# Both halves of an inverse transform copied out of PSUM in one step, with a new order of all operations

## The chip, the cores and the metric

The kernel runs on one core of a Trainium2 chip. The metric is the device time in microseconds (us) of one execution. The engines are TensorE (PE in the profile, its weight loads PEld), VectorE (DVE), ScalarE (ACT), GpSimd (POOL) and SyncE (SP). PE writes its results to PSUM, which has eight banks; every result has to be copied out by ACT or DVE before its bank can be used again.

## The reference

Sparse attention (8 global keys and a local window of 96) is followed by a gated long convolution that is computed with a Fourier transform along the sequence. Shapes: q, k, v are 4 x 8 x 768 x 64, the output is 4 x 768 x 512.

```python
scores = scale * q @ k^T - slope[h] * distance      # only kept keys: pos < 8, or 0 <= rel < 96
a = softmax(scores); x = (a @ v) as [B, S, 512]
x1, x2, x3 = split(x @ w_proj)                      # 512 columns each
conv = irfft(rfft(x2, axis=seq) * rfft(filter, axis=seq))
out = (x1 * conv * x3) @ w_out
```

## The kernel before

The work goes batch by batch, four of them; while one batch is in its convolution, the next is in its attention. Per batch the stages are:

- load q and k (DMAs that GpSimd issues, L347), turn them with TensorE (L704, L707; operations "q" and "k") and copy the result to QT and KT (L322);
- scores of two heads (a head pair) against a group of two or three key tiles (L756, operation "scores"). The contraction is over 64 rows, so two matmuls, one on each half of the array, go side by side. A group is evacuated by one ACT exponential (L771) from two banks and, except in batch 0, multiplied by a mask on DVE (L788). In batch 0 each group also has a bias matmul over 128 rows ahead of it (L750, operation "near");
- values (L806, L811), division by the row sum (L830 on DVE or L834 on ACT, into xn), transposition (L852) and a copy to xT (L322);
- gates: x1 and x3, from xT and w (L932; copies L326 or L942, product L946);
- projection of the folded sequence (L997; copies to ab, L322), forward transform (L1163; copies to X), products with the filter's transform (L1181 to L1201);
- inverse transform, `conv`, L1028 and L1035: for each of four column tiles a matrix for the even part and one for the odd part, four matmuls of 128 columns each (operation "inv"). Each goes to a bank of its own, 384 columns wide, and is copied to the tile `eo` (L322);
- recombination on DVE (L1120 to L1126, `mixed`), then the gate (L1140 to L1145, `gated`), the output projection (L1090, operation "out"), its copy to `ot` (L326 or L328) and the store.

`Plan` records some 980 operations with what they read, write and hold. Nothing is scheduled at run time: the string `ORDER` (L41) lists all operations as number, engine letter (P, A, V, G, S) and, for those that take PSUM banks, the banks' numbers. `i2` with a bank is a filler of two matmuls without use (L318). `Plan.schedule` follows the list, so each engine's queue is what the list says, and an engine that waits for its next operation does nothing else. With each operation the list also chooses between ACT and DVE where both can do it.

What the program joins in one step is told by tuples of batch numbers: with `PAIR_X` two banks of the forward transform are copied by one instruction of 1024 columns, and with `PAIR_EO` the even and the odd half of an inverse would be copied by one instruction of 768 columns. `PAIR_EO` is empty, so there are 32 copies of 384 columns. The lines that take the one way or the other (in `conv`):

```python
both = [g.bank(), g.bank()] if b in self.PAIR_EO else None
...
g.op("P", ..., turn, acq=[bk] if not both else () if par else both, use=[bk] if both and par else (), ...)
if both and par == 0:
    continue
if both:
    g.op("AV", self.evac(2 * h), lambda e, ...: self.copy(e, eo[:, jj], both[0].two()[:, :, 0:h]), use=both, ...)
    continue
g.op("AV", self.evac(h), lambda e, ...: self.copy(e, eo[:, jj, par], bk.f32()[:, 0:h]), use=[bk], ...)
```

Of the kernel before, what the change touches and what calls it, by code (L numbers as in the profile page):

```python
# [42 lines left out]
50G 82P0 19V 12A 23V 58S 34G 57V 49A 47V 51G 24V 80P6 52G 35V 25A 86P2 13V 71G 20A 14V 81A 83V 60G 198P7 15A 36A 62G
41A 92P0 203V 200V 37V 59G 87V 94P1 79A 64G 202V 43A 206V 84P6 93A 63G 199V 96P45 95V 76A 61G 88P0 201A 97A 205V
146P23 85V 65G 74A 90P1 204V 40A 42V 39A 102P45 91V 89A 152P67 147A 38V 28V 115P01 103A 26V 207V 98P23 153A 27V 208V
236G 100P45 99A 209V 148P67 233G 116A 119P23 210V 149A 231G 211V 120A 104P01 235G 117P67 212V 101A 230G 105V 113P23
106V 118A 232G 150P45 213V 114A 107P67 234G 124P01 151A 108V 109V 154P23 229G 72A 214V 110P5 66G 111P 125V 73A 155V
121P67 126V 221P4 242G 30A 156V 159P01 222A 67G 122V 77A 157P2 112V 335P3 238G 158A 160V 217P4 123V 215P5 336A 240G
161V 127P2 333P6 218A 128P 237G 334V 329P3 216A 219P0 129V 241G 75A 331P6 330V 369P45 220A 162P1 332V 244G 134P7
370A 163V 239G 366P23 189V 345P01 136A 130P4 346A 190V 243G 223P67 191V 367A 68G 192V 226P01 193V 135P5 227A 451G  # L50
347V 228A 348P23 194V 165P0 132V 245G 349A 137V 131P1 78A 69G 195V 337P2 350V 225A 403P45 70G 181V 164P3 224A 338V
456G 404A 341P7 180V 168P2 248G 342A 182V 169P6 133V 170A 183V 249G 406P45 166A 371V 343P1 407A 339P7 184V 251G
142P2 171V 344A 340V 138P3 250G 246S 167V 144A 409P67 247S 412P45 252G 185V 410A 351P01 186V 139P2 187V 450G 352A
140V 143P6 196V 413A 172P7 141V 353V 375P01 174A 372P23 414V 354P45 373A 253G 255P7 188V 368V 376A 267P2 462G 197V
256A 411V 457G 259P1 355A 377V 374V 463G 257P7 268A 356V 260A 405V 279P45 452G 258A 280P 357P23 145V 281A 378P01
408V 455G 269P7 358V 379V 359A 380V 453G 381P45 282V 261P01 458G 262P 382V 271P6 383V 263A 454G 283V 360P23 272A
176P4 471G 264V 270A 555P5 361V 265V 178A 470G 415P01 556A 362V 273P67 461G 274P 416V 173P4 417V 275A 464G 551P5
549P2 175V 552A 363P3 465G 550V 364P 420P01 276V 365A 460G 586P45 277V 565P67 587A 459G 384P2 421V 385P 266V 177P3
566A 254G 422V 561P4 553P5 386A 693G 418P6 278V 623P01 419A 423P7 562V 674G 395P2 424A 179V 298P6 685G 554V 624A
563P4 391P7 442V 397A 683G 396P3 299A 441V 564A 557P5 466G 294P0 398V 387P1 558A 443V 682G 286P2 559P3 393A 444V  # L60
568P45 287A 681G 560V 399P6 295A 569A 288P0 445V 592P23 290P7 588V 389A 392P4 671G 593A 570V 400P1 446V 677G 291A
394V 296P5 401A 429P2 447V 297A 472G 289A 589P67 402V 284P3 431A 686S 473G 292P5 449V 590A 388P4 448V 469G 574P01
285A 632P67 567V 293A 468S 489P2 633A 689G 625V 467S 390V 425P3 575A 680G 591V 626P45 427A 571P67 301V 433P0 474G
627A 672S 300V 437P1 687S 572A 634V 684G 426P3 673S 302V 490A 675G 595P45 576V 439A 629P67 596A 475P2 303V 676G 573V
435A 491P1 304V 678G 630A 594V 580P45 476A 305V 670G 438P0 492A 581V 487P2 631V 582A 688G 440V 577P67 428V 691G
493P01 494P 597V 479P3 488A 306V 679G 495A 499P45 578V 628V 500P 477P2 501A 307V 598P01 478A 579V 601P45 690G 480A
599V 583P7 502V 600A 584P 430P6 602V 692G 771S 603V 434P2 503V 773S 481P45 585A 482P 432V 604P3 605P 308V 635P01
483A 769S 640P67 496V 606A 636V 314P4 497V 768S 637A 641V 485V 311P5 642V 770S 619P3 498V 607P6 315A 777S 436V 638P7
312A 514P0 484V 615P1 621A 309V 639A 643P2 317P3 775S 617A 486V 515A 518P7 644A 506P1 310V 516P0 510P4 609A 774S
504P2 519A 508P5 662V 620P6 505A 318A 616P7 661V 772S 507A 781P23 509A 618V 608P1 511A 663V 779S 782A 512P7 320P5  # L70
622V 513A 610V 517A 780S 784P23 664V 790P67 321A 657P0 521V 785A 611P1 778S 665V 659A 808P45 520V 791A 323P3 776S
666V 809A 522V 787P67 645P0 324A 792V 313S 788A 706P5 523V 667V 613A 805P23 783V 802P67 707A 612P1 668V 803A 326P4
789V 647A 614V 806A 849P67 524V 846P01 694P5 850A 669V 807V 847A 852P23 710P6 525V 695A 804V 327A 708P7 526V 711A
328S 810V 811P01 853A 325S 843P45 851V 696P6 319S 709A 529V 316S 844A 796P23 322S 698P7 797V 812A 854V 798V 712P45
713P 699A 718P01 786V 719P 697A 653P2 530V 720A 700P67 701P 646P3 813V 714A 848V 649P1 648V 655A 860P45 702A 527V
793P23 651A 654P0 861V 721V 862A 658P1 794V 656V 817P67 795V 543P0 660V 818V 845V 546P1 819A 722V 814P23 528V 855P45
547A 815V 703V 537P6 816A 856V 704V 799P7 800P 857V 650P1 801A 863P2 715V 820P3 858P4 864A 821P 705V 531P5 859A 716V
822A 735P2 652V 723P4 534P7 717V 724A 544A 727P1 886V 725P4 736A 737P3 545S 733P0 532A 834P2 885V 548S 726A 839P5
728A 887V 738A 729P4 734A 731P1 888V 838P3 730A 732A 889V 823P0 840A 739V 890A 828P4 740V 906P1 836A 891V 825A 894P2
538A 741V 892V 540P0 742A 893V 866P3 830A 743V 907A 896P6 541A 744V 898P4 895A 542S 745V 897A 539S 918P01 535A 748V  # L80
919P 533S 908P2 899A 536S 746V 920A 900P67 901P 829P4 749V 902A 910P0 921V 909A 871P1 911A 903V 912P67 841A 904V
913P 833P0 914A 922V 824P2 905V 831A 865P5 835A 916V 826A 923P4 942P7 915V 938P0 943A 927P2 762P6 917V 924A 928A
842V 925P4 939A 747V 929P2 926A 870P7 930A 837V 944P4 940P0 932V 945A 750P2 931V 941A 933V 763A 756P4 946V 751A 947V
832V 934A 765P0 948V 827V 949A 935V 753P2 757A 936V 950V 867A 880P6 758S 951V 873A 937V 754A 876P4 952V 766A 953V
759P5 755S 882A 752S 955V 868A 875P0 767S 954V 760A 764S 956V 881P6 877A 761S 968V 878A 957P1 872A 966V 883A 879V
963P0 958A 874V 869V 884V 960P5 959S 964A 967V 969V 965S 974P4 961A 975P 962S 970P1 976A 971P 977S 978P0 972A 979P
# [1258 lines left out]
```

## Time and profile before

| | |
|---|---|
| time, median of 3 runs | 164.04 us (164.03 to 164.37) |
| the profiled execution's own time | 163.79 us |
| its span, first to last instruction | 162.0 us |
| PE busy | 153.5 us, 1587 matmuls |
| DVE busy | 151.2 us, 358 instructions |
| ACT busy | 153.6 us, 318 instructions |
| POOL busy | 77.1 us, 101 instructions |
| mean granted TensorE clock | 0.997 |

A busy time counts an instruction from its start to its end, and neighbours on one engine overlap: what an instruction costs its engine is the distance from its start to the start of the next. In the timeline a row merges neighbours of one form: the first column is the start of the first, the second the time until the end of the last, xN their number. The distance between two rows' first columns, divided by N, is then the cost of one. In the list of waits the columns are the total, the number and the longest wait in us; a wait of PEld for "issue" is one that no semaphore explains.

### The profile page before, as it was taken

What the parts mean: (1) busy time and instruction counts of PE and PEld (TensorE: products, weight loads), DVE (VectorE), ACT (ScalarE), POOL (GpSimd) and SP (SyncE); (2) the same over time, 40 slices, a digit from 0 to 9 for tenths busy, and PEclk for the clock granted to TensorE, in tenths of its full rate; (3) what the DMA queues carried; (4) which work ended last, traced back from release to release, by engine and by line L of the source; (5) the groups of instructions that cost most, each with busy time, mean ns of one, the idle gap of its engine ahead of it and who ended that gap; (6) DMA issues with size and microseconds to landing.
All of it is one profiled execution on the core that took longest, in us unless ns stands there. A gap on an engine that the chain in (4) does not pass through costs nothing.

```text
span 162.0 us, 4215 instructions
## 1 busy us (share of the span) xinstructions
PE 153.5 (95%) x1587; PEld 92.7 (57%) x1587; DVE 151.2 (93%) x358; ACT 153.6 (95%) x318; POOL 77.1 (48%) x101
## 2 busy tenths in 40 slices
PE   4879899999999999999999999999999999999990
PEld 1564238756656687764568565445666754574550
DVE  6799898999999999999999999999999999999941
ACT  7999899999999999999999999999999999999970
POOL 7999199989978999999971000000000000000000
PEclk9999999999999999999999999999999999999998
DMA  4999999999999999999999984707000303300775
GB/s 169 213 154 148 168 150 152 153 158 165 178 165 150 136 137 138 154 153 163 163 94 152 103 160 99 121 13 296 27 4 6 129 0 126 135 4 0 302 282 195
DMA packets 84956, 21.95 MB, mean 135 GB/s; under 512 B 75584, under 2 KB 81992, under 8 KB 84936
## 3 DMA queue, kind: packets, MB, share of 16 engines
q0 software_dynamic: 73040, 12.11, 104.5%
q1 hardware_dynamic: 11896, 9.57, 22.4%
q8 instruction: 12, 0.20, 0.5%
q14 instruction: 8, 0.07, 0.1%
HBM read 25.40 MB, written 6.29 MB: 196 GB/s over the span
## 4 chain that ended last, share of the span: by engine, by line
PE 86%; ACT 4%; POOL 3%; issue 2%; DVE 1%; POOLq 0%
PE bank L932 26%; PE bank L997 13%; PE bank L1090 12%; PE bank L756 7%; PE bank L806 4%; PE bank L852 4%; PE bank L811 4%; PE bank L1028 3%; PE bank L704 3%; PE bank L1163 3%; PE bank L750 3%; ACT mask L624 1%; PE bank L1035 1%; POOL qn L347 1%; PE bank L687 1%
## 5 line engine op out<-in xcount | busy, mean ns | idle before, releaser
L932 PE MATMUL bank<-xT,w 128*128 128x384 f16 x256 | 48.6, 326 | 0.0
L771 ACT ACTIVATE E<-bank 128x864 f16<-128x864 f32 x48 | 42.0, 930 | 0.9 <-PE bank L756 0.8
L932 PEld LDWEIGHTS <-w 128*128 128x128 f16 x256 | 23.3, 98 | 15.7 <-issue 1.6
L347 POOL DMA_DIRECT2D vn<-in_v_dram x28 | 25.7, 937 | 2.0 <-DMA w<-in_moe_w_proj_dram 0.9
L347 POOL DMA_DIRECT2D kn<-in_k_dram x25 | 21.7, 886 | 4.6 <-DMA vn<-in_v_dram 3.6
L1090 PE MATMUL bank<-wo,y 128*128 128x512 f16 (+1 forms) x100 | 23.0, 370 | 0.0
L347 POOL DMA_DIRECT2D qn<-in_q_dram x25 | 22.1, 891 | 1.0 <-PE bank L673 0.5
L788 DVE TENSOR_TENSOR E<-E,mask 128x864 f16<-128x864 f16 x36 | 20.7, 596 | 0.0
L326 ACT ACTIVATE x<-bank 128x384 f16<-128x384 f32 x30 | 16.5, 552 | 0.1
L997 PE MATMUL bank<-w,xs 128*128 128x512 f16 x64 | 16.0, 379 | 0.0
L322 ACT CAST eo<-bank 128x384 f16<-128x384 f32 x32 | 15.3, 594 | 0.5 <-ACT g L942 0.3
L326 ACT ACTIVATE ot<-bank 128x512 f32<-128x512 f32 x23 | 14.7, 665 | 1.0 <-PE bank L1090 1.0
L756 PE MATMUL bank<-QT,KT 64*128 64x216 f16 (+2 forms) x224 | 15.2, 245 | 0.0
L806 PEld LDWEIGHTS <-E 128*128 128x128 f16 x224 | 13.9, 97 | 2.0 <-issue 0.2
L806 PE MATMUL bank<-vn,E 128*128 128x65 f16 x224 | 14.9, 193 | 0.0
L811 PE MATMUL bank<-vn,E 128*128 128x65 f16 x192 | 14.7, 193 | 0.0
L834 ACT ACTIVATE xn<-bank,rc 128x64 f16<-128x64 f32 x64 | 14.1, 407 | 0.2 <-DVE rc L835 0.2
L1090 PEld LDWEIGHTS <-y 128*128 128x128 f16 x100 | 9.2, 98 | 8.7 <-issue 0.2
L322 ACT CAST ab<-bank 128x512 f16<-128x512 f32 x24 | 14.0, 628 | 0.0
L756 PEld LDWEIGHTS <-KT 64*128 64x128 f16 x224 | 7.6, 94 | 11.2 <-issue 10.0
L811 PEld LDWEIGHTS <-E 128*128 128x128 f16 x192 | 13.1, 97 | 0.6
L830 DVE TENSOR_TENSOR xn<-bank,rc 128x512 f16<-128x512 f32 (+1 forms) x17 | 13.0, 776 | 0.2
(158 smaller groups left out, 329.9 us busy)
## 6 DMA issues: line engine op xcount, KB each, us to landing
out_dram<-ot SPq DMA_DIRECT2D x23, 256.0 KB
vn<-in_v_dram POOLq DMA_DIRECT2D x28, 120.0 KB, 7.7
kn<-in_k_dram POOLq DMA_DIRECT2D x16, 96.0 KB, 5.1
qn<-in_q_dram POOLq DMA_DIRECT2D x16, 96.0 KB, 5.1
w<-in_moe_w_proj_dram POOLq DMA_DIRECT2D x4, 256.0 KB, 5.8
kn<-in_k_dram POOLq DMA_DIRECT2D x7, 120.0 KB, 6.8
g<-in_moe_filter_fft_dram POOLq DMA_DIRECT2D x1, 768.0 KB, 9.9
qn<-in_q_dram POOLq DMA_DIRECT2D x6, 128.0 KB, 7.9
```

The lines of the kernel that those rows point to most:

```text
L322: {"A": nc.scalar.copy, "V": nc.vector.tensor_copy, "G": nc.gpsimd.tensor_copy}[e](out, in_)
L326: self.nc.scalar.mul(out, in_, c)
L347: return self.g.op(eng, 0.57 + 0.00035 * nbytes[0] if eng == "G" else 0.5, lambda _: e.dma_start(dst, src), w=w, r=r, nbytes=nbytes, name= ...
L756: nc.tensor.matmul(bs[hh].f32()[:, off:off + w], self.KT[hs, hp, P * m:P * m + P], self.QT[hs, hp, KL * m:KL * m + w], start=(off == 0 and ...
L771: g.op("A", act(864), lambda _: nc.scalar.activation(eo, bs[0].two()[:, :, 0:432].rearrange("p h (m w) -> p h m w", m=2), Act.Exp, scale=s ...
L788: g.op("V", dve(864, 2), lambda _: nc.vector.tensor_mul(eo, eo, mk), r=[("mask", 2 * hp), ("mask", 2 * hp + 1)], w=[("E", hp, gi)], name=" ...
L806: nc.tensor.matmul(o[:, n, hh], ef[:, at:at + P], vt[:, t, 2 * hp + hh, 0:D + 1], start=first, stop=(t == 0), skip_group_check=True)
L811: nc.tensor.matmul(o[:, n, hh], ef[:, at:at + P], vt[:, t - 1, 2 * hp + hh, 0:D + 1], start=False, stop=True, skip_group_check=True)
L834: nc.scalar.mul(to[:, i, n], o[:, i, n, 0:D], rc[:, i, n])
L932: nc.tensor.matmul(bk.f32()[:, 0:h], self.w[:, c, o + P * j:o + P * j + P], self.xT[:, c, h * s:h * s + h], start=(c == 0), stop=(c == 3))
L997: nc.tensor.matmul(bk.f32(), src[:, c], w[:, c, DM:2 * DM], start=(c == 0), stop=(c == 3))
L1090: nc.tensor.matmul(bk.f32()[:, 0:n], y[:, c, P * t:P * t + P], self.wo[:, c, cs], start=(c == 0), stop=(c == 3))
```

## The change

`PAIR_EO` holds all four batches now: the first inverse matrix of a pair takes both banks, the second writes to the other one, and one instruction of 768 columns copies both. So 32 copies of 384 columns become 16 of 768, and sixteen operations fall away. `ORDER` was made anew for that; the planner that made it (it isn't part of the kernel) now counts DVE's waits behind GpSimd's DMA issues. The list is one line shorter, so a line of the kernel after has a number lower by one.

```diff
 ORDER = """
-44S 3G 1V 4V 46S 31G 5V 0V 55S 2A 8A i2b0 9V 48S 7V 10A 16P6 54G 32V 21P1 45A 53G 17A 11P7 6G 18V 22A 33V 56A 29V
...
+44S 3G 1V 4V 46S 31G 5V 0V 21P5 55S 2A 29A 8V 48S 16P4 7V 22A 30V 11P2 54G 17A 23V 45A i2b1 53G 24V 12A 33V 6G 18V
...
     PAIR_X = (0,1,2,3)
-    PAIR_EO = ()
+    PAIR_EO = (0,1,2,3)
     PAIR_OT = ()
```

PE keeps its 1587 matmuls and GpSimd and SyncE keep the order of all their instructions. What moves is the order on PE, ACT and DVE, the banks, and the choice between ACT and DVE: ACT has 19 instructions fewer, DVE 4 fewer. Among them ACT takes four QT copies and two KT copies more, and three copies to xT, two fillings of E with constants and one scaling xn (eight instructions, L834) fewer; DVE has the other side of each.

The first place is PE in the attention of batch 3. In the rows, L756 (L755 after) is a matmul of scores with its weight load, L932 (L931 after) one of a gate; `bank_105` to `bank_108` are the four pairs of banks. Before:

```order
L932 LDWEIGHTS w
L932 MATMUL bank_108<-xT,w 128x384
L756 LDWEIGHTS KT
L756 MATMUL bank_106<-QT,KT 128x216
L756 LDWEIGHTS KT
L756 MATMUL bank_106<-QT,KT 128x216
L756 LDWEIGHTS KT
L756 MATMUL bank_106<-QT,KT 128x216
L756 LDWEIGHTS KT
L756 MATMUL bank_106<-QT,KT 128x216
L932 LDWEIGHTS w
L932 MATMUL bank_105<-xT,w 128x384
```

One group of scores stands alone between gates. After, at the end of the first run of scores in that attention:

```order
L755 LDWEIGHTS KT
L755 MATMUL bank_106<-QT,KT 128x216
L755 LDWEIGHTS KT
L755 MATMUL bank_106<-QT,KT 128x216
L755 LDWEIGHTS KT
L755 MATMUL bank_108<-QT,KT 128x216
L755 LDWEIGHTS KT
L755 MATMUL bank_108<-QT,KT 128x216
L755 LDWEIGHTS KT
L755 MATMUL bank_108<-QT,KT 128x216
L755 LDWEIGHTS KT
L755 MATMUL bank_108<-QT,KT 128x216
```

Here the group in `bank_106` is followed by the one in `bank_108` with nothing between. Over the whole of PE's order, the 36 groups of scores of batches 1 to 3 stand in 23 runs before and in 17 after: 7, 8 and 8 in the three batches before, 7, 5 and 5 after.

The second place is ACT at the inverse transform of the last batch. `eo<-bank` is the copy of an inverse, `ot<-bank` one of an output, `uw<-uw` a step of the recombination. Before:

```order
L942 CAST g_88<-bank_106 128x384
L322 CAST eo<-bank_108 128x384
L322 CAST eo<-bank_107 128x384
L322 CAST eo<-bank_106 128x384
L322 CAST eo<-bank_105 128x384
L322 CAST eo<-bank_107 128x384
L322 CAST eo<-bank_106 128x384
L322 CAST eo<-bank_107 128x384
L322 CAST eo<-bank_105 128x384
L326 ACTIVATE ot<-bank_108 128x512
L326 ACTIVATE ot<-bank_106 128x512
```

After:

```order
L941 CAST g_88<-bank_107 128x384
L325 ACTIVATE x_94<-bank_107 128x384
L941 CAST g_88<-bank_105 128x384
L321 CAST eo<-bank_106 128x768
L321 CAST eo<-bank_107 128x768
L321 CAST eo<-bank_108 128x768
L321 CAST eo<-bank_105 128x768
L325 ACTIVATE uw<-uw 128x4x128
L325 ACTIVATE ot<-bank_107 128x512
```

Eight copies have become four, each from another pair of banks, and the recombination's step now comes right behind them.

The third place is the head of ACT's queue. `E<-uw` fills a part of E with constants, `vn<-uw` a part of vn with ones; `y<-bank` is the first step of the sine tables, `kn<-h`, `qn<-h` and `kn<-pp` are casts of the first loads. Before:

```order
L444 ACTIVATE warm<-warm 1x2
L337 ACTIVATE E<-uw 128x2x6x32
L337 ACTIVATE E<-uw 128x2x80
L337 ACTIVATE E<-uw 128x2x6x32
L337 ACTIVATE E<-uw 128x2x80
L322 CAST kn<-h_85 128x768
L491 ACTIVATE y<-bank_108 128x256
L491 ACTIVATE y<-bank_105 128x512
L322 CAST vn_63<-X 8x8x64
L491 ACTIVATE y<-bank_108 128x512
L322 CAST kn<-pp 128x768
L501 ACTIVATE fold<-y 128x512
```

After:

```order
L443 ACTIVATE warm<-warm 1x2
L336 ACTIVATE vn_63<-uw 128x8x32
L336 ACTIVATE vn_63<-uw 128x48x2
L490 ACTIVATE y<-bank_107 128x512
L490 ACTIVATE y<-bank_107 128x256
L321 CAST kn<-h_85 128x768
L490 ACTIVATE y<-bank_106 128x512
L500 ACTIVATE fold<-y 128x512
L321 CAST qn<-h_86 128x768
L500 ACTIVATE fwd<-y 128x256
L325 ACTIVATE eo<-ident 128x128 x2
L321 COPY p_84<-fwd 128x512
```

The tables' steps now come ahead of most casts and of all fillings of E, which went to DVE.

More of the change, by code (lines that the diff above doesn't have):

```diff
@@ L41 @@
 ORDER = """
-44S 3G 1V 4V 46S 31G 5V 0V 55S 2A 8A i2b0 9V 48S 7V 10A 16P6 54G 32V 21P1 45A 53G 17A 11P7 6G 18V 22A 33V 56A 29V
[L43 to L86, printed above, removed]
@@ L87 @@
-982P7 980V 983P 973S 984V 981S 985S
+44S 3G 1V 4V 46S 31G 5V 0V 21P5 55S 2A 29A 8V 48S 16P4 7V 22A 30V 11P2 54G 17A 23V 45A i2b1 53G 24V 12A 33V 6G 18V
+25A 19V 50G 82P1 47A 13V 32V 34G 20A 80P0 38A 51G 41A 26A 198P4 14V 52G 83A 36V 92P5 56V 71G 15A 204V 58S 200V 49V
+81A 60G 35V 86P7 37A 10V 62G 39V 96P01 203V 27V 59G 206V 73A 84P6 64G 201V 72A 202V 57V 9V 93A 113P23 63G 199V 205V
+42V 97A 90P4 87V 61G 94P5 114A 88P0 65G 85V 91A 89V 98P23 76A 115P67 95V 43A 99A 148P01 116A 40V 152P45 28V 207V
@@ new lines @@
+149A 208V 236G 100P23 77A 102P01 209V 233G 153A 150P67 210V 103A 119P45 231G 211V 151A 104P01 235G 212V 120A 146P67
+105V 230G 106V 101A 117P45 213V 232G 147A 107P01 234G 121P23 118A 108V 214V 154P67 229G 74A 122V 109V 219P4 66G 78A
+110P5 123V 111P 223P01 220A 242G 155V 112V 159P23 224A 156V 67G 225A 124P45 75A 215P0 238G 125V 160V 331P1 126V 216A
+226P67 240G 161V 332A 329P4 127P5 128P 237G 330V 157P0 227A 325P1 158V 228A 162P2 241G 129V 327P4 326A 217P0 180V
+244G 134P5 163A 328V 218A 221P1 239G 190V 136A 399P67 362P23 181V 222A 243G 130P0 189V 400A 182V 68G 341P45 131P1
@@ new lines @@
+132A 191V 447G 363A 183V 164P0 192V 342A 245G 344P67 193V 135P2 133V 345A 69G 364V 402P45 337P1 194V 403A 70G 333P7
+195V 168P6 137V 166A 452G 169P3 338A 184V 248G 185V 170A 365P45 196V 339P2 334A 171V 335P6 249G 165P0 197V 366A 336V
+142P3 251G 340A 167V 138P5 246S 250G 346V 144A 371P67 247S 186V 140A 350P23 252G 401V 368P01 372A 139P4 187V 351A
+446G 367V 143P5 141V 369A 172P6 145V 347P23 404V 174A 408P45 405P01 188V 79A 253G 267P6 370V 348A 343V 458G 255P7
+406A 373V 453G 349V 257P3 256A 407V 409A 459G 353P01 352V 259P2 268A 354V 410V 258A 448G 279P45 355V 280P 356P67
@@ new lines @@
+281A 451G 269P3 357V 358V 260A 449G 377P01 282V 270A 261P45 262P 454G 378V 283V 374P67 263A 541P2 379V 450G 271P3
+542A 375V 264V 467G 547P0 376V 272A 173P1 548A 466G 265V 273P45 274P 175V 411P67 275A 457G 266V 359P2 543P1 460G
+412V 276V 360P 544A 416P45 413V 461G 176P3 361A 456G 417V 277V 557P01 578P67 178A 418V 380P2 455G 579A 381P 177P3
+278V 254G 558A 615P45 414P7 179V 685G 419P6 616A 415V 287P01 288P 382V 545P3 420A 284P45 617V 666G 285P 289A 395P2
+437V 286A 293P67 677G 294P 438V 555P0 397A 290P45 546A 675G 291P 383P1 559V 295A 440V 553P2 462G 551P3 385A 439V
@@ new lines @@
+387P6 554A 674G 552V 391P1 292A 441V 673G 392P2 393A 296V 384P4 389A 663G 394V 556A 549P5 386V 560P67 669G 618P23
+442V 550A 624P01 297V 421P4 561A 468G 443V 483P5 423A 678S 298V 469G 619A 396P6 445V 465G 625A 471P4 398V 464S 580V
+484A 681G 563P67 463S 621P01 444V 472A 566P23 388P5 672G 564A 299V 626V 487P4 567A 470G 565V 429P6 664S 390V 622A
+676G 300V 679S 422P7 488A 623V 665S 667G 581P01 431A 584P23 301V 587P45 582A 485P6 668G 562V 588A 424V 475P0 670G
+583V 486A 302V 433P1 585A 662G 568V 569P45 476A 489P67 589V 680G 490P 435A 572P23 570V 586V 491A 473P0 683G 573V
@@ new lines @@
+571V 574A 430P1 492V 425P6 620V 671G 590P45 303V 427A 495P23 474A 496P 593P67 591V 432V 497A 426P0 594V 592V 682G
+434P1 595A 428V 477P23 304V 478P 684G 759S 632P45 436V 479A 575P0 761S 576P 633V 498V 596P1 597P 577A 627P67 493V
+757S 499V 598A 307P3 628V 634V 629A 313P0 756S 481V 310P2 480V 758S 599P1 305V 635P4 314A 630P5 482V 601A 603P6 765S
+636A 494V 611P7 631A 306V 607P0 308A 763S 311A 608P1 654V 613A 509P45 609A 510P 653V 506P23 605A 762S 507P 612P0
+511A 610V 500P67 508A 655V 501P 760S 503P45 504P 656V 502A 316P1 614V 505A 767S 772P23 657V 778P67 317A 600P0 513V
@@ new lines @@
+779A 768S 322P5 512V 773A 602V 645P4 658V 766S 323A 796P01 780V 775P23 647A 769P67 659V 797A 637P5 764S 514V 604P4
+776A 798V 638P0 770A 515V 309S 606V 793P23 324S 639A 516V 790P67 794A 698P4 640V 791A 517V 649P5 777V 699A 840P01
+831P23 660V 651A 799P67 686P4 841A 518V 661V 832A 319P5 792V 800A 688P0 842V 320A 521V 834P23 689A 837P67 321S 702P1
+771V 687A 315S 835A 801V 312S 710P45 711P 522V 318S 690P0 703A 838A 833V 784P23 700P1 836V 691A 839V 712A 692P67
+785V 693P 795V 538P0 701A 786V 694A 704P45 774V 705P 848P23 519V 539A 781P67 706A 843P01 849V 782V 520V 850A 646P4
@@ new lines @@
+783V 535P5 648V 696V 805P67 650P4 844V 806V 536A 695V 802P23 807A 537S 845V 529P5 540S 803V 652V 846P0 641P1 804A
+708V 642P4 713V 707V 851P7 787P6 643A 788P 714V 808P2 852A 809P 526P1 847V 810A 697V 523P0 789A 709V 724P23 644V
+527A 725P 718P67 874V 719P 726A 854P1 720A 873V 721P23 722P 827P4 856A 875V 723A 715P67 716P 876V 811P1 717A 877V
+822P2 829A 727V 878A 882P6 728V 894P3 530A 879V 883A 729V 859P4 895A 880V 906P67 730A 907P 532P3 881V 908A 731V
+886P5 732V 813A 884P6 887A 733V 824A 898P1 885A 736V 861A 888P67 533A 889P 909V 896P2 890A 534S 737V 869P4 531S 897A
@@ new lines @@
+891V 826P3 899A 892V 900P67 828A 901P 816P1 910V 902A 893V 750P5 524A 903V 812P6 871A 525S 904V 818A 821P4 528S 751A
+905V 817P0 814A 823A 734V 914P23 819A 915P 911P45 912P 825V 916A 927P01 815V 924P67 820V 925P 735V 928P 913A 863P2
+926A 917V 753P3 830V 929A 918V 738P4 919V 930V 920A 858P5 931V 739A 932V 744P6 921V 933A 922V 754A 741P0 934V 860A
+923V 935V 745A 853P4 937V 742A 746S 747P1 936V 855A 743S 939V 864P0 740S 748A 938V 755S 868P4 940V 752S 950V 941P1
+749S 870A 862V 866A 857V 947P6 872V 865A 952V 942A 944P5 867V 948A 951V 943S 953V 949S 958P7 945A 959P 946S 954P4
@@ L88 @@
+960V 955P 962P7 961S 956A 963P 966P3 964V 967P 957S 968A 965S 969S
 """
```

## The prediction

> **What bounds the kernel now.** I read the page first, then the list of waits by stage, then PE's timeline. The page's first part and its chain:
>
> ```profile
> span 162.0 us, 4215 instructions
> PE 153.5 (95%) x1587; PEld 92.7 (57%) x1587; DVE 151.2 (93%) x358; ACT 153.6 (95%) x318; POOL 77.1 (48%) x101
> ...
> PE 86%; ACT 4%; POOL 3%; issue 2%; DVE 1%; POOLq 0%
> ```
>
> Three engines look equally full, so the shares decide nothing; the chain gives 86% of the span to PE. To test that, I asked for PE's own waits between 20 and 158 us. The answer has its heading and not one row. What is left stands with its weight loads, whose first row in the same stretch is by far the largest:
>
> ```profile
> PEld L756 <- issue: 7.5, 21, 0.4
> ```
>
> So from 20 us on PE waits for nobody. Its only gaps lie around the scores (L756), and no semaphore explains them. ACT in turn waits for PE there, which is how an engine looks that has room:
>
> ```profile
> ACT E L771 <- PE bank L756: 0.8, 2, 0.6
> ```
>
> The end is therefore: the time at which PE has become dense, plus PE's work from there, plus a tail. The tail:
>
> ```profile
> 155.69 2.55 PE L1090 MATMUL bank<-wo,y 128*128 128x512 f16 x15
> 157.89 0.80 DVE L328 TENSOR_SCALAR ot<-bank 128x256 f32<-128x256 f32 x2 [2.23 <-ACT ot L326]
> ```
>
> PE ends at 155.69 + 2.55 = 158.24, the span at 162.0: 3.8 us for the last copies and stores, whose pieces the new list keeps. What saves time must shorten PE's work or make PE dense sooner. 1 us is then 1 us.
>
> **Part 1: fewer runs of scores.** PE's timeline gives the price of a run:
>
> ```profile
> 36.36 1.47 PE L932 MATMUL bank<-xT,w 128*128 128x384 f16 x8
> 37.67 0.50 PE L704 MATMUL bank<-ident,qn 128*128 128x128 f16 x6
> ...
> 97.17 0.36 PE L756 MATMUL bank<-QT,KT 64*128 64x216 f16 x4
> 97.46 0.82 PE L932 MATMUL bank<-xT,w 128*128 128x384 f16 x4
> ...
> 99.30 0.54 PE L756 MATMUL bank<-QT,KT 64*128 64x216 f16 x8
> 99.78 1.47 PE L932 MATMUL bank<-xT,w 128*128 128x384 f16 x8
> 101.18 0.36 PE L756 MATMUL bank<-QT,KT 64*128 64x216 f16 x4
> 101.47 1.04 PE L1090 MATMUL bank<-wo,y 128*128 128x512 f16 x4
> ```
>
> Eight gate matmuls take 37.67 - 36.36 = 1.31 us up to a transposition, but 101.18 - 99.78 = 1.40 up to scores: going in costs 0.09. One group alone takes 97.46 - 97.17 = 0.29, two together 99.78 - 99.30 = 0.48, so the second costs 0.19 and going out 0.10. A run that is joined to another saves 0.09 + 0.10, about 0.2 us of PE. The order has 23 runs before and 17 after: 6 x 0.2 = 1.2 us. As PE is dense in batches 2 and 3, where the six go, nothing hides this. PE's other work is the same 1587 matmuls. The ends are 1.1 (0.19 each) and 1.4 (0.23 each: the list's 7.5 us over 21 gaps are even 0.36 each, but hold time in which the last matmul still runs).
>
> Longer runs hold more banks: three groups hold six of the eight until ACT has made three exponentials. Five of the ten runs in batches 2 and 3 are such. Batch 1 already has two of them:
>
> ```profile
> 43.20 0.77 PE L756 MATMUL bank<-QT,KT 64*128 64x216 f16 x16
> 43.91 2.12 PE L932 MATMUL bank<-xT,w 128*128 128x384 f16 x12
> 45.96 0.73 PE L756 MATMUL bank<-QT,KT 64*128 64x216 f16 x12
> 46.62 1.68 PE L997 MATMUL bank<-w,xo 128*128 128x512 f16 x7
> ...
> 16.58 2.69 ACT L771 ACTIVATE E<-bank 128x864 f16<-128x864 f32 x3
> ```
>
> After both PE goes straight on (a gate matmul is 1.31 / 8 = 0.164, 43.91 + 12 x 0.164 = 45.88, and the next run starts at 45.96 with its usual 0.1). So I charge them nothing. Without that cover a wait for one exponential would come back per run: 2.69 / 3 = 0.9 us by the last row, from ACT, 4.5 us for five runs.
>
> **Part 2: the joined copies.** The form's row, and four rows of ACT's timeline:
>
> ```profile
> L322 ACT CAST eo<-bank 128x384 f16<-128x384 f32 x32 | 15.3, 594 | 0.5 <-ACT g L942 0.3 <-PE bank L1035 0.2
> ...
> 65.56 0.89 ACT L322 COPY QT<-bank 128x768 f16<-128x768 f16 x1
> 66.25 0.59 ACT L326 ACTIVATE x<-bank 128x384 f16<-128x384 f32 x1
> 66.63 0.96 ACT L322 CAST eo<-bank 128x384 f16<-128x384 f32 x2
> 67.36 1.03 ACT L771 ACTIVATE E<-bank 128x864 f16<-128x864 f32 x1
> ```
>
> By the mean of 594 ns one would hope for 0.3 us per pair. But starts count: two small copies occupy ACT for 67.36 - 66.63 = 0.73 us, and one of 768 columns (QT, the nearest row) for 66.25 - 65.56 = 0.69. A pair saves 0.04, sixteen 0.6 us of ACT, and ACT isn't what PE waits for: I book nothing. What the joining may cost is bank time. The even half can't be copied until the odd one is done:
>
> ```profile
> 94.38 0.28 PE L1028 MATMUL bank<-inv,X 128*128 128x128 f16 x2
> 94.60 0.27 PE L1028 MATMUL bank<-inv,X 128*128 128x128 f16 x2
> ```
>
> One matrix takes 94.60 - 94.38 = 0.22. A bank was held for 0.22 + 0.37 and both are now held for 0.44 + 0.69 = 1.13. Where PE's next matmul needs one of the two at once, it waits longer by at most 0.69 - 0.37 = 0.32. The four pairs of the last batch go to four different pairs of banks in the new order, so I book nothing here either. The other moves (four QT copies and two KT copies more on ACT, eight scalings and two fillings fewer) shift work of the order of 1 us between two engines that both have room.
>
> **Part 3: the head.** Here PE does wait:
>
> ```profile
> 9.39 0.59 PE L546 MATMUL bank<-ident,fold 128*128 128x128 f16 x4 [0.99 <-DVE y L497]
> 16.72 0.54 PE L750 MATMUL bank<-eo 128*128 128x432 bf16 x2 [0.78 <-ACT QT L322]
> 2.15 1.65 ACT L337 ACTIVATE E<-uw 128x384 f16<-128x384 f16 x4
> 7.63 0.71 POOL L347 DMA_DIRECT2D kn<-in_k_dram  x1
> 7.84 0.78 DVE L494 TENSOR_SCALAR y<-y 128x512 f32<-128x512 f32 x1
> DVE pp L636 <- DMA g<-in_moe_filter_fft_dram: 0.4, 1, 0.4
> ```
>
> The first wait is for the sine tables, the second for a QT copy on ACT. The tables' steps on ACT came behind 1.65 us of E fillings and the first cast. Now the ones (two short fillings) stand there, two of the tables' three copies come ahead of the first cast, and the inverse tables' matmuls (L546) stand behind two transpositions and not three. The DVE step at 7.84 ended late, at 8.62, 0.28 after GpSimd's issue ended (7.63 + 0.71 = 8.34): this is the wait that the planner now knows. With all this gone PE would gain 0.99 + 0.78 = 1.8. But DVE gets the E fillings, and it has to wait for the filter's DMA (last row) in both kernels, whose issue stands in the same place. A later load sets a hard limit:
>
> ```profile
> L347 POOL DMA_DIRECT2D w<-in_moe_w_proj_dram x5: 770/812/834, 26.4 to 38.3; - x5
> w<-in_moe_w_proj_dram POOLq DMA_DIRECT2D x1, 512.0 KB, 7.6
> ```
>
> The projection's weights are issued last of the five, at 38.3, and land at 38.3 + 7.6 = 45.9. PE first needs them at 46.62. GpSimd's order is unchanged and it is busy throughout, so PE can lead by 0.7 us there and no more. Ends: a gain of 0.7, or a loss of 0.4 (a second wait like the one at 7.84, with DVE fuller). I take 0.5, nearer to the limit, since ACT's head is shorter by 1 us.
>
> **The sum.** 1.2 (runs) + 0.5 (head) - 0.1 (some new waits of PE, of which the order before has none) = 1.6 us. The profiled execution has 163.79, 1.8 over its span, and would have 162.2; the median of the three runs, 164.04, lies 0.25 above it, and becomes 162.4.
>
> **Rivals.** (a) **Slower: the pairs of banks hold PE up.** Place: the sixteen inverse pairs. Price: up to 0.32 us each, 5.2 in all; at half of that 2.6, and the time is 164.04 - 1.6 + 2.6 = 165.0. It decides from 0.1 us per pair. For it: ACT, at 95%, copies late whenever it is behind. Against: PE's empty list of waits. [...] Chance of the slower side: 0.11.
>
> (b) **ACT is the bound after all**, its 153.6 us being the page's longest. Then only the copies count: 164.04 - 0.6 = 163.4. Against it: its wait for PE of 0.8 us. [...] Chance 0.08.
>
> (c) **The new list doesn't do what it promises**: the head gains nothing, and the longer runs give back half of the 1.2: 164.04 - 0.6 = 163.4. For it: the loads leave 0.7 us. Against: the two runs of batch 1. Chance 0.16, and 0.03 for no change at all, from waits that eat just what is gained.
>
> **How the numbers follow.** My forecast, 162.4, has 0.62. About 0.2% (0.33 us) is what a measurement of this kernel can tell from no change. Faster takes the forecast, most of (b) and (c): 0.80; same 0.09; slower 0.11. The forecast's own ends are 1.4 + 0.7 = 2.1 (162.0, or 161.6 with the runs' own spread of 0.3) and 1.1 - 0.4 = 0.7 (163.4). The range goes on to 164.0 for what (b) and (c) may lose beyond that, and leaves out (a).
>
> **What would show it.** Right: in the profile after, PE's list of waits from 20 us on is still empty, the issue gaps before L755 fall by six, PE ends near 156.6, and the last weights' projection starts no earlier than 45.9. Wrong: waits of PE for `eo` copies or exponentials (a, c), waits of PE's weight loads for the w load, or ACT without any wait for PE (b).

## The result and the profile after

| | before | after |
|---|---|---|
| time, median of 4 runs | 164.19 us (164.03 to 164.37) | 162.59 us (162.4 to 162.69) |
| profiled execution, own time | 163.79 us | 162.59 us |
| PE's last matmul ends | 158.24 us | 157.10 us |
| span | 162.0 us | 160.8 us |

The ratio is 0.9885, with a 95% interval of 0.9856 to 0.9914: 1.6 us faster by the medians, 1.2 between the two profiled executions (that of before lay 0.4 below its median). Ratios leave disturbed runs out; one profile below, of the run with the last two weights moved, is of a disturbed run, and only the place of a wait and the clock behind it are read from it.

The page of the kernel after, first part and chain:

```profile
span 160.8 us, 4208 instructions
PE 151.4 (94%) x1587; PEld 91.8 (57%) x1587; DVE 150.3 (93%) x354; ACT 152.1 (95%) x299; POOL 77.1 (48%) x101
...
PE 71%; ACT 11%; POOL 9%; DMA 3%; issue 3%; DVE 0%; POOLq 0%
```

All three full engines lost busy time: PE 2.1 us, ACT 1.5, DVE 0.9. PE's share of the chain, 86% before, is now 71%, and ACT, GpSimd and a DMA have more of it.

PE's own wait and some of those of its weight loads in the kernel after, 20 to 158 us:

```profile
PE bank L931 <- DMA w<-in_moe_w_proj_dram: 0.3, 1, 0.3
...
PEld L755 <- issue: 6.7, 20, 0.4
PEld L931 <- DMA w<-in_moe_w_proj_dram: 1.2, 3, 0.5
...
PEld L1089 <- DVE y L1144: 0.8, 2, 0.4
...
PEld L703 <- DMA qn<-in_q_dram: 0.5, 1, 0.5
PEld L755 <- DVE KT L321: 0.4, 1, 0.4
```

Before, PE itself had no wait in this stretch, and its weight loads had none for a load or for y. Now PE waits for weights, and its weight loads wait besides for a load of q and, at the end, for DVE's gated y. So PE ran up against others in several places.

How far PE is ahead can be read at three points. The last group of batch 0's scores, before and then after:

```profile
24.42 0.36 PE L756 MATMUL bank<-QT,KT 64*128 64x216 f16 x6
```

```profile
23.50 0.36 PE L755 MATMUL bank<-QT,KT 64*128 64x216 f16 x4
...
43.54 2.12 PE L931 MATMUL bank<-xT,w 128*128 128x384 f16 x12 [0.25 <-DMA w<-in_moe_w_proj_dram]
46.26 1.90 PE L996 MATMUL bank<-w,xo 128*128 128x512 f16 x8
...
153.70 3.40 PE L1089 MATMUL bank<-wo,y 128*128 128x512 f16 x18
```

At the end of the head PE is 24.42 - 23.50 = 0.92 us ahead. At the projection it is 46.62 - 46.26 = 0.36: of the rest the gates' wait for w at 43.5 us took 0.25, and smaller waits, for w, the load of q and copies to KT, lie before it. At its end (153.70 + 3.40 = 157.10) it is 1.14 ahead. Between the projection and the end PE gained 0.78 us, where the six runs of scores were to give 1.2.

The busy times by 20 us for the kernel before (the columns are the stretch, then busy time and count of PE, PEld, DVE, ACT and POOL, the granted clock, the DMA share and GB/s), which the prediction did not use:

```profile
60.00:80.00 20.00, 20.00 (x211) 12.81 (x209) 20.00 (x43) 20.00 (x38) 19.50 (x23) 1.00 2.09 154
80.00:100.00 20.00, 20.00 (x235) 12.97 (x233) 19.76 (x41) 20.00 (x56) 4.55 (x6) 1.00 1.98 124
100.00:120.00 20.00, 20.00 (x188) 10.64 (x187) 19.79 (x42) 19.99 (x42) 0.00 (x0) 1.00 0.36 100
```

From 60 to 120 us not only PE is full but ACT (59.99 of 60) and DVE (59.55 of 60) as well. PE's empty list of waits says that PE is always just in time, not that the others have room. The experiments test this.

### The profile page after: what moved, and what is told of

Same layout as the page of the kernel before. It is cut to its first block, busy times and chain, and to the rows that moved or that the text cites. A ratio compares the mean times of both kernels' runs of the same rounds, so it can differ in the third digit from the quotient of the medians.

```text
span 160.8 us, 4208 instructions
## 1 busy us (share of the span) xinstructions
PE 151.4 (94%) x1587; PEld 91.8 (57%) x1587; DVE 150.3 (93%) x354; ACT 152.1 (95%) x299; POOL 77.1 (48%) x101
## 4 chain that ended last, share of the span: by engine, by line
PE 71%; ACT 11%; POOL 9%; DMA 3%; issue 3%; DVE 0%; POOLq 0%
PE bank L931 22%; PE bank L996 13%; PE bank L1089 13%; PE bank L755 4%; POOL qn L346 4%; POOL kn L346 4%; DMA w<-in_moe_w_proj_dram 3%; PE bank L1027 3%; PE bank L1162 3%; PE bank L805 3%; ACT E L770 3%; PE bank L851 3%; PE bank L810 3%; PE bank L703 2%; ACT mask L623 2%
## 5 line engine op out<-in xcount | busy, mean ns | idle before, releaser
L931 PE MATMUL bank<-xT,w 128*128 128x384 f16 x256 | 48.4, 326 | 0.3 <-DMA w<-in_moe_w_proj_dram 0.3
L931 PEld LDWEIGHTS <-w 128*128 128x128 f16 x256 | 23.5, 98 | 16.7 <-DMA w<-in_moe_w_proj_dram 1.2
L346 POOL DMA_DIRECT2D qn<-in_q_dram x25 | 21.5, 870 | 1.6 <-PE bank L1034 0.5
L325 ACT ACTIVATE x<-bank 128x384 f16<-128x384 f32 x32 | 17.7, 579 | 1.0 <-PE bank L931 0.9
L325 ACT ACTIVATE ot<-bank 128x512 f32<-128x512 f32 (+1 forms) x23 | 14.9, 666 | 2.2 <-PE bank L1089 2.1
L805 PE MATMUL bank<-vn,E 128*128 128x65 f16 x224 | 15.2, 193 | 0.0
L810 PE MATMUL bank<-vn,E 128*128 128x65 f16 x192 | 15.0, 193 | 0.0
L321 ACT CAST ab<-bank 128x512 f16<-128x512 f32 x24 | 14.8, 658 | 0.0
L755 PE MATMUL bank<-QT,KT 64*128 64x216 f16 (+2 forms) x224 | 14.2, 242 | 0.5 <-DVE QT L321 0.4
L945 DVE TENSOR_TENSOR g<-bank,x 128x384 f16<-128x384 f32 x24 | 13.1, 548 | 0.9 <-PE bank L755 0.6
L755 PEld LDWEIGHTS <-KT 64*128 64x128 f16 x224 | 7.8, 94 | 10.4 <-issue 9.2
L829 DVE TENSOR_TENSOR xn<-bank,rc 128x512 f16<-128x512 f32 (+1 forms) x18 | 13.5, 761 | 0.1
L321 ACT CAST X<-bank 128x1024 f16<-128x1024 f32 x12 | 13.0, 1081 | 0.3 <-PE bank L1162 0.2
```

The costliest lines, as they stand in the source:

```text
L321: {"A": nc.scalar.copy, "V": nc.vector.tensor_copy, "G": nc.gpsimd.tensor_copy}[e](out, in_)
L325: self.nc.scalar.mul(out, in_, c)
L346: return self.g.op(eng, 0.57 + 0.00035 * nbytes[0] if eng == "G" else 0.5, lambda _: e.dma_start(dst, src), w=w, r=r, nbytes=nbytes, name= ...
L755: nc.tensor.matmul(bs[hh].f32()[:, off:off + w], self.KT[hs, hp, P * m:P * m + P], self.QT[hs, hp, KL * m:KL * m + w], start=(off == 0 and ...
L805: nc.tensor.matmul(o[:, n, hh], ef[:, at:at + P], vt[:, t, 2 * hp + hh, 0:D + 1], start=first, stop=(t == 0), skip_group_check=True)
L810: nc.tensor.matmul(o[:, n, hh], ef[:, at:at + P], vt[:, t - 1, 2 * hp + hh, 0:D + 1], start=False, stop=True, skip_group_check=True)
```

## The experiments

The kernel before had medians of 164.00 to 164.19 us beside all the runs, so medians can be compared with 162.59 for the kernel after. But that one rests on four runs, and by its ratio, 0.9885, it would be 162.1 to 162.3 beside these medians. What is added to the kernel after may therefore cost some 0.4 us more than the medians say, so the traces are set side by side too, at the end of this section.

**Only the joining undone.** The new order with two copies of 384 columns in the place of each one of 768:

```diff
-    PAIR_EO = (0,1,2,3)
+    PAIR_EO = ()
...
-284P45 617V 666G 285P ... 286A
+284P4 625V 674G 286P5 ... 285A 287A
```

> The changed kernel with only the joining undone: the same new order, but each of the sixteen inverse pairs is copied out of PSUM by two ACT instructions of 384 columns, one behind the other in the place of the one of 768. Theory 1 (PE's work is the bound; runs of scores and the head made the gain): ACT gets 16 x 0.04 = 0.6 us of work off the path and the even bank comes free earlier, so 162.6 as the changed kernel, within 0.3. [...] Rival 3 (the pairs hold PE up in the changed kernel, which is why its PE loses 0.5 us between 95 and 140 us): 162.1.

163.04 us (162.79 to 163.66), ratio to before 0.9942 (0.9917 to 0.9966). The joining is worth about 0.45 us by the medians, 0.9 by the ratios. Rival 3 falls: with the even bank free earlier the kernel is slower, so what the pairs hold up, if anything, is less than what the sixteen copies cost. The page of this kernel has:

```profile
PE 151.5 (94%) x1587; PEld 91.9 (57%) x1587; DVE 150.8 (94%) x354; ACT 152.9 (95%) x315; POOL 76.9 (48%) x101
```

ACT has 16 instructions and 0.8 us of busy time more, PE the same. At least half of the ACT time that the split copies cost is seen in the end, which theory 1 did not expect of an engine with room. At the 0.04 us per copy that the rows of ACT's timeline give, all of it seen, the time would be 162.59 + 0.6 = 163.2.

**Matmuls between blocks.** 19 fillers of one 128x128 matmul on PE, where no run of scores begins or ends (`i101` is a filler of one such matmul):

```diff
-143P5
+i101b5 143P5
```

> The changed kernel with 19 idle matmuls of 128x128 added on PE between 32 and 111 us, each between two blocks of 128-row matmuls (no switch), into a bank that the next block overwrites. They are about 0.055 us each, 1.04 us of PE. Theory 1 (PE is the bound): all of it is seen, 162.6 + 1.0 = 163.6. Rival 2 (ACT is the bound): at most 0.2, 162.8.

163.05 us (162.74 to 163.73), ratio 0.9944 (0.9918 to 0.9970). The fillers are as cheap as thought, which this kernel's timeline shows at one of them:

```profile
105.27 0.22 PE L318 MATMUL bank<-ident 128*128 128x128 f16 x1
105.32 0.81 PE L934 MATMUL bank<-xT,w 128*128 128x384 f16 x4
```

By the starts in the trace they take 0.056 us each, 1.06 in all; 0.46 are seen by the medians, 1.0 by the ratios. Four of the 19 stand ahead of the projection, where the kernel after waits for weights in any case, and cost nothing: the projection starts at 46.26 us in both traces. PE's last matmul ends at 157.59, 0.49 us later than in the kernel after, so of the other 15, 0.84 us in all, 0.49 is seen. That is not an engine with room; whether it alone sets the end, this run doesn't decide.

**Matmuls within runs.** The same 19 fillers, each between two groups of one run of scores:

```diff
-399P67 362P23
+399P67 i101b2 362P23
```

> The changed kernel with the same 19 idle matmuls of 128x128 as in the run with matmuls between blocks (163.05), but each between two groups of one run of scores, so that 17 runs become 36. Theory 1 (a switch in and out costs 0.19 us of PE): 162.6 + 19 x (0.055 + 0.19) = 167.2; with PE's first half microsecond covered, as in that run, 166.7. Rival 2 (runs have no price of their own): as that run, 163.05.

166.83 us (166.47 to 167.72), ratio 1.0176 (1.0134 to 1.0217). Against the fillers between blocks that is 166.83 - 163.05 = 3.78 us for 19 more runs, 0.20 us each: theory 1's price of a run. This kernel's timeline in batch 3 shows where it goes:

```profile
103.92 0.36 PE L758 MATMUL bank<-QT,KT 64*128 64x216 f16 x4
104.21 0.23 PE L318 MATMUL bank<-ident 128*128 128x128 f16 x1
104.38 0.36 PE L758 MATMUL bank<-QT,KT 64*128 64x216 f16 x4
```

A group takes 0.29 up to the filler (0.19 inside a run), the filler 0.17 up to the next group (0.05 between blocks): 0.10 out and 0.12 in. Of these 0.22 us on PE 0.20 are seen in the end.

**The runs split by moving blocks.** No filler; ten blocks that stood ahead of a run now stand behind its first group:

```diff
-138P5 246S 250G 346V 144A 371P67
+246S 250G 346V 144A 371P67 138P5
```

> The changed kernel with the same instructions, but ten matmul blocks (gate, projection, output) that stand just ahead of a run of scores are put behind the first group of that run, so that 17 runs become 27; nothing is added, and each moved block starts 0.2 us later. Theory 1: ten more switches in and out at 0.19 us: 162.6 + 1.9 = 164.5, slower than the kernel before the change (ends 164.3 and 164.9). Rival 2 (ACT's copies are the gain): no change, 162.6. Rival 3 (a run's price is hidden by waits that PE has anyway): about half, 163.5.

166.75 us (166.75 to 167.11), ratio 1.0167 (1.0139 to 1.0195): 4.2 us and not 1.9. Ten runs at 0.20 are 2.0. The other 2.2 were not measured singly; the waits point to the blocks' own delay. ACT's largest and PE's in this kernel, 20 to 158 us:

```profile
ACT x L324 <- PE bank L930: 3.1, 6, 0.8
ACT ab L320 <- PE bank L995: 1.1, 2, 0.8
```

```profile
PE bank L754 <- ACT E L769: 0.9, 3, 0.3
PE bank L754 <- DVE g L944: 0.7, 1, 0.7
PE bank L754 <- ACT KT L320: 0.6, 2, 0.4
```

A gate that comes late makes ACT wait for its x, and later scores then wait for ACT and DVE. Theory 1's price fits, its sum doesn't: moved work seems to have a cost of its own where nobody has room.

**Idle copies on ACT, in the kernel after and in the one before.** 12 copies of 128x128 between 63 and about 145 us in each, to a tile that nobody reads:

```diff
+        self.g.extra = lambda e: self.copy(e, self.scr, self.ident)
...
-286A
+xA 286A
```

After:

> The changed kernel with 12 idle copies of 128x128 within SBUF added on ACT, spread from 63 to 142 us, 0.20 us each by the fillings of the same size, 2.4 us of ACT. Rival 2 (ACT is the bound): 162.6 + 2.4 = 165.0. Theory 1 (PE is the bound and ACT has room): under 0.6 of it is seen, 162.6 to 163.2; not nothing, as the changed kernel's PE already shows small waits between 95 and 140 us.

Before:

> The kernel before the change with 12 idle copies of 128x128 within SBUF added on ACT between about 63 and 142 us, 0.20 us each, 2.4 us in all (the same that cost the changed kernel 1.7 us). Theory 1 (in the kernel before, PE alone is the bound and ACT has room, as the prediction said): at most 0.4 is seen, 164.0 to 164.4. Theory 4 (PE and ACT are level from 60 to 120 us in the kernel before as well; the empty list of PE's waits hides that ACT is just behind): 1.0 to 1.8 are seen, 165.0 to 165.8.

After: 164.31 us (163.95 to 164.71), ratio 1.0009 (0.9988 to 1.0029). Before: 165.3 us (165.01 to 165.99), ratio 1.0084 (1.0052 to 1.0116). ACT's timeline at two of the copies in the kernel after with them:

```profile
62.61 0.40 ACT L327 COPY scr<-ident 128x128 f16<-128x128 f16 x1
62.81 0.91 ACT L327 CAST eo<-bank 128x768 f16<-128x768 f32 x1
...
99.83 0.65 ACT L327 COPY scr<-ident 128x128 f16<-128x128 f16 x1
100.01 1.25 ACT L776 ACTIVATE E<-bank 128x864 f16<-128x864 f32 x1
```

All twelve take 0.18 to 0.20 us from their start to that of the next instruction, whatever that is: ACT had its next work waiting each time. Of 12 x 0.2 = 2.4 us the kernel after shows 1.7, the kernel before 1.3 (2.0 and 1.4 by the ratios). The first falls between the theories (165.0, and 162.6 to 163.2), the second within theory 4's 1.0 to 1.8. Theory 1 falls, for the kernel before as well.

**Idle copies on DVE** in the kernel after, 24 in pairs, in the same way:

> The changed kernel with 24 idle copies of 128x128 within SBUF added on DVE, in pairs at twelve places from about 63 to 142 us; by the DVE rows of that size 0.1 to 0.17 us each, 2.4 to 4 us. Theory 1 (PE alone is the bound): under 0.5 is seen, below 163.1. Theory 4 (PE and ACT are level, DVE has room): the same, below 163.1. Theory 9 (all three are level): over half of it, 164 to 165.5.

166.48 us (165.8 to 166.74), ratio 1.0143 (1.0105 to 1.0182), 3.9 us more. DVE's timeline at the first pair and at the costliest, then the chain of this kernel:

```profile
63.78 0.41 DVE L327 COPY scr<-ident 128x128 f16<-128x128 f16 x2
64.11 0.95 DVE L875 TENSOR_TENSOR xab<-xT 128x1536 f16<-128x1536 f16 x1
...
78.79 0.85 DVE L327 COPY scr<-ident 128x128 f16<-128x128 f16 x2
79.56 0.55 DVE L951 TENSOR_TENSOR g<-bank,x 128x384 f16<-128x384 f32 x1
```

```profile
DVE 54%; PE 12%; ACT 12%; DMA 9%; issue 7%; POOL 5%; DVEq 0%; POOLq 0%; ACTq 0%
```

A pair takes 0.33 us as a rule, but 0.70 and 0.77 in two places; by the starts in the trace the twelve add up to 4.65 us, and 3.9 of it is seen. DVE now carries 54% of the chain. 166.48 lies above every range named, even theory 9's 164 to 165.5, as the pairs cost more than the 2.4 to 4 us expected. Theories 1 and 4 fall, and theory 9's share, over half, holds: DVE has as little room as the others.

**The head alone.** The kernel before with the order after up to 26 us:

```diff
-44S 3G 1V 4V 46S 31G 5V 0V 55S 2A 8A i2b0 ...
+44S 3G 1V 4V 46S 31G 5V 0V 21P5 55S 2A 29A ...
```

> The kernel before the change with the changed kernel's order up to about 26 us on every engine and its own order behind that (copies not joined, 23 runs of scores). Theory 1 (the head is a term of its own, 0.5 us, limited by the projection's weights): 164.05 - 0.5 = 163.55, from 163.3 to 163.8. Rival 5 (the head's lead is lost again since ACT is level with PE from 60 us): 164.05, within 0.2. Rival 6 (the head is most of the gain): 162.8 or less.

164.85 us (164.5 to 165.88), ratio 1.005 (1.002 to 1.008): slower, which no theory gave. Its waits from 20 to 60 us, first PE's, then ACT's:

```profile
PE bank L685 <- DVE xn L828: 0.6, 1, 0.6
PE bank L804 <- DVE xn L828: 0.3, 1, 0.3
```

```profile
ACT h L324 <- PE bank L685: 1.2, 1, 1.2
ACT xT L320 <- PE bank L850: 0.8, 1, 0.8
```

From 60 us on PE's list is empty again. PE starts the projection at 47.70 us, 1.08 later than in the kernel before, and takes as long from there: the loss lies just behind the seam, where what follows was ordered for the old head. So this run says nothing on the head; this piece of the order couldn't be tried without what follows it.

**The head taken back.** The kernel after with 1.0 us of idle matmuls on PE at the end of the head:

```diff
-117P45
+i118b4 117P45
```

> The changed kernel with 18 idle matmuls of 128x128 (about 1.0 us of PE) added once, ahead of the last near group at about 22 us, where PE has just become dense: it takes back what the new head gained on PE there. Theory 1 (the head's lead of about 0.95 is cut to half by the waits for the projection's weights): the waits for w shrink and half of the microsecond is seen, 163.1. Rival 5 (the head is worth nothing, ACT is level later on): 162.6 to 162.8. Rival 6 (the whole lead counts): 163.6.

162.89 us; eight of nine runs lie between 162.87 and 162.93, the ninth, the profiled one, at 165.12. By the medians 0.3 of the 1.0 us is seen (0.7 by the ratio, 0.993, 0.9907 to 0.9953). It lies between rival 5 and theory 1. The only trace is that of the run at 165.12, so that it is the weights' waits that absorb the rest was not seen. And the matmuls take back PE's lead alone, not what the new head may have brought ACT and DVE.

**Three of the five loads of the weights issued first** (GpSimd's order):

```diff
-208V 236G ... 219P4 66G 78A ... 156V 67G 225A ... 182V 68G 341P45
+208V 66G 67G 68G 236G ... 219P4 78A ... 156V 225A ... 182V 341P45
```

> The changed kernel with three of the five loads of the projection's weights (w0, w1024, w256) issued in GpSimd's idle gap at 16.2 us, ahead of the loads of batch 1; all later issues keep their order, so the last two weights are issued about 2.4 us earlier. The waits of PE's weight loads for w (1.2 us in three) should go. Theory 1 (PE is the bound, the lead of the head is cut to half by these waits): 162.6 - 0.5 = 162.1. Theory 4 (PE and ACT are level later on): PE keeps the lead until 60 us, ACT does not, and the time stays at 162.6, within 0.2. Rival 7 (the loads of batch 1 are now late): slower, 163.

167.91 us (166.0 to 168.29 but for one run at 306; 167.59 without that run), ratio 1.0208 (1.0163 to 1.0254). That is rival 7's side, and far more than its 163. PE's timeline of this kernel where loads of batch 1 are late:

```profile
30.87 0.49 PE L702 MATMUL bank<-ident,kn 128*128 128x128 f16 x6 [1.98 <-DMA kn<-in_k_dram]
...
32.81 0.58 PE L702 MATMUL bank<-ident,qn 128*128 128x128 f16 x6 [1.01 <-DMA qn<-in_q_dram]
```

**The last two weights two issues earlier:**

```diff
-191V 447G ... 345A 69G 364V ... 403A 70G 333P7
+191V 69G 70G 447G ... 345A 364V ... 403A 333P7
```

> The changed kernel with only this moved: the issues of the last two loads of the projection's weights (w1280 and w512) stand on GpSimd ahead of one load of q for batch 2 and one of v for batch 1, so they go out about 1.7 us earlier and those two loads about 1.6 us later. The waits of PE's weight loads for w at 43.5 us should go. Theory 1 (PE alone is the bound, so the lead that these waits cost is worth its full time): 162.6 - 0.5 = 162.1. Theory 4 (PE and ACT are level from 60 us): a lead of PE alone buys little, 162.4 to 162.6. Rival 7 (as in the run with three weights moved, a load that is now later holds PE up): 163 or more.

164.71 us, but from 163.16 to 167.0 in twelve runs; ratio 1.0001 (0.9968 to 1.0034). None was as fast as the kernel after. PE's timeline in the profiled one, at 167.0:

```profile
51.70 0.22 PE L804 MATMUL bank<-vn,E 128*128 128x65 f16 x2 [2.49 <-DMA vn<-in_v_dram]
```

The wait for w is gone, and one for a load of v is there. This is one run; the next kernel, with the same weights moved, has neither wait in its profile, so what holds up the faster of these twelve is not shown. The sure finding is that moving loads forward made neither kernel faster.

**That, with two runs of scores fewer:**

```diff
-243G 130P0 189V ... 193V 135P2 133V
+341P45 130P0 131P1 ... 402P45 135P2 337P1
```

> The run above with, besides, two gate blocks of batch 1 put behind the score group that followed them, so that 17 runs of scores become 15, no instruction more or less. Theory 1: another 2 x 0.2 = 0.4 us, 161.7. Theory 4: about half of that over the run above, 0.2. Rival 8 (the joined group waits for a bank whose exponential is not done): no gain, or 0.3 slower.

163.91 us (162.73 to 166.54), ratio 0.9979 (0.9954 to 1.0004); not faster than the kernel after. Against the run that it is built on it is 0.4 us faster by the ratios, but their intervals overlap: that doesn't tell theory 1's 0.4 from theory 4's 0.2 or rival 8's nothing. Waits of PE and of its weight loads in it, 20 to 60 us:

```profile
PE bank L804 <- ACT E L769: 0.6, 1, 0.6
PE bank L754 <- ACT E L769: 0.5, 1, 0.5
```

```profile
PEld L804 <- DVE E L786: 1.1, 1, 1.1
```

No wait for w, but some for exponentials and masks, as rival 8 has it. No experiment gave a kernel faster than the one after.

**The same stretch in every trace.** From the start of the projection (L997 in the kernel before) to the end of PE's last matmul, in us. "Put in" is the work added behind the start of the projection, from the starts in the traces:

| kernel | projection starts | PE ends | stretch | put in | more than without it |
|---|---|---|---|---|---|
| before | 46.62 | 158.24 | 111.62 | | |
| after | 46.26 | 157.10 | 110.84 | | |
| joining undone | 45.95 | 157.55 | 111.60 | ACT 0.8 busy | 0.76 |
| matmuls between blocks | 46.26 | 157.59 | 111.33 | PE 0.84 (15) | 0.49 |
| matmuls within runs | 47.57 | 161.66 | 114.09 | PE 3.9 (14) | 3.25 |
| copies on ACT, after | 45.97 | 158.81 | 112.84 | ACT 2.35 | 2.00 |
| copies on ACT, before | 46.56 | 159.91 | 113.35 | ACT 2.36 | 1.73 |
| copies on DVE | 46.15 | 161.15 | 115.00 | DVE 4.65 | 4.16 |
| head alone | 47.70 | 159.30 | 111.60 | | |

Of a microsecond put in behind the projection 0.6 to 0.8 is seen on PE, 0.85 on ACT (0.7 in the kernel before) and 0.9 on DVE; on ACT it is 0.7 if only the ends are compared (158.81 - 157.10 = 1.71 of 2.35). These are three engines that are about level. And with the copies split the stretch is as long as in the kernel before, though it has six runs of scores fewer. PE started 0.31 us earlier there than in the kernel after, and may have lost that again because ACT and DVE were not ahead with it; so the joining is worth 0.45 to 0.76 us of the 0.78 gained behind the projection.

## Why the prediction was right, point by point

**The number.** 162.4 was forecast, 162.59 came; the profiled execution was to have 162.2 and has 162.59. The tail is 160.8 - 157.10 = 3.7 us, as said.

**What bounds the kernel.** Here the argument failed, at the step "ACT in turn waits for PE there, which is how an engine looks that has room". The row had 0.8 us in two waits over 120 us or more, and it was read as if it held everywhere. Asked by stage, ACT's waits in the kernel before are, from 20 to 60 us and then from 60 to 140 us:

```profile
ACT E L771 <- PE bank L756: 0.8, 2, 0.6
ACT xn L834 <- DVE rc L835: 0.2, 1, 0.2
```

```profile
ACT uw L326 <- DVE mix L1122: 0.2, 1, 0.2
```

In the middle ACT never waits for PE. The shares "equally full", which the prediction set aside, were the truth: a microsecond added in the middle of the kernel after shows 0.6 to 0.8 us on PE, 0.7 to 0.85 on ACT and 0.9 on DVE. "1 us is then 1 us" is nearly as true of ACT and DVE, which were booked as having room. The number came out all the same, as the change took time from all three.

**Part 1, the runs.** The price of 0.2 us is shown (3.78 us for 19). But this is the term that was furthest off: six runs fewer were to bring 1.2 us, and behind the projection, where all six lie, PE gained 0.78, of which the joining has 0.45 to 0.76. At most 0.3 is left for the runs and all else that the order changed there. That a run saved brings less than a run added costs fits engines that are level; no run shows the six by themselves. The sign that was to show it, six issue gaps fewer, did not come: the rows go from 21 to 20, and with 19 runs more (the fillers within runs) there are 18. That row does not count runs.

**Part 2, the joined copies.** Booked at nothing, and mis-sized: 0.45 us by the medians, up to 0.76 by the traces. The 0.6 us of ACT was a good estimate; that it lay off the path was wrong. The bank time cost nothing that can be seen, as booked, and rival (a)'s place is empty: PE's list after has no wait for a copy to `eo`.

**Part 3, the head.** The mechanism was right. Both waits that it names are gone; PE has a new one there, for a table's copy on DVE, whose queue has two fillings of E shortly before it:

```profile
13.62 0.86 PE L706 MATMUL bank<-ident,kn 128*64 128x128 f16 x24 [1.60 <-DVE inr L327]
```

PE came out of the head 0.92 us earlier, and the loads cut that to 0.36 at the projection, which starts at 46.26, not before 45.9. But the load that bit was an earlier one, for the gates at 43.5 us. So 0.36 came of the 0.5 that was booked; taking 1.0 us of PE's lead back costs 0.3 by the medians.

**The sum** had 1.2 for the runs, 0.5 for the head and nothing for the copies. By the traces the 1.2 us between the two profiled executions are 0.36 ahead of the projection, 0.78 behind it (the copies 0.45 to 0.76, the runs and the rest what is left) and 0.06 in the tail (3.76 before, 3.70 after). The other 0.4 of the medians' 1.6 is the profiled execution before, which lay that much below its median. So that the total came out was in good part luck: a term of nothing that brought 0.45 or more made up for much of what the runs fell short by. Two slips changed nothing: sixteen times 0.32 is 5.1, not 5.2, and the ends of the forecast are 161.9 and 163.3. Rival (b) had the engine half right: ACT bounds along with PE, not in its place, and its 163.4 was not the time.

**The signs named ahead.** PE's list was to stay empty: it has one wait of 0.3. PE was to end near 156.6: it ended at 157.10. Of the signs for "wrong", the weight loads' wait for w came (1.2 us), and ACT has no wait at all for PE between 60 and 140 us.

## What to carry to other kernels

An empty list of waits shows that an engine is never kept waiting, not that it is alone: look at the busy time of all engines by stage, and if several are full, put 2 us or more of idle work on each in turn (1 us drowned in the runs' spread here); its visible share is the price of a microsecond there. Where the order on PE stays the same, compare the traces at the same matmul: that was steadier than the medians. In such a kernel a change pays if it takes time from all the full engines (here 2.1, 1.5 and 0.9 us of busy time went, for 1.6 us by the medians), and moving work in the order can cost even where nothing is added (some 2.2 us beyond the price of the runs with the ten blocks moved). A lead won early is worth little if the loads behind it come no sooner (here 0.36 of 0.92 us was left).
